# Key sums joined to the attention visit of the unit ahead, and second weights split a step sooner

## Chip, cores and metric

The kernel runs on one core of one Trainium2 chip. The metric is the time of one execution on the device in microseconds; a kernel's time is the median of its runs. Beside the times there is one profiled execution, and all views of the profile come from it.

## What is computed

An attention block with a polynomial sketch, and behind it a mixture of four experts. The essence of the reference:

```python
def phi(x):                       # x: (4, 4, 1088, 32)
    a = np.einsum('rd,bhsd->bhsr', S1, x)       # r = 8
    b = np.einsum('rd,bhsd->bhsr', S2, x)
    return np.einsum('bhsi,bhsj->bhsij', a, b).reshape(*x.shape[:-1], 64)
q_p, k_p = phi(q), phi(k)
kv = np.einsum('bhsf,bhsd->bhfd', k_p, v)
z = np.sum(k_p, axis=2)
attn = np.einsum('bhsf,bhfd->bhsd', q_p, kv) / (np.einsum('bhsf,bhf->bhs', q_p, z)[..., None] + 1e-6)
x = attn.transpose(0, 2, 1, 3).reshape(4352, 128)
p = domain_probs / (domain_probs.sum(-1, keepdims=True) + 1e-9)
out = sum(p[:, e:e+1] * (np.maximum(x @ w1[e], 0) @ w2[e]) for e in range(4))   # w1: 128 x 1024
```

All inputs and the output are float32.

## The kernel before

**The experts are the backbone.** The 4352 rows of x are cut into 11 chunks, `CHUNKS = [128, 448, 512, 448 x 7, 128]`. For each chunk `m` there are `NQ = 16` steps, four per expert `e`, each with two blocks `j` of 128 hidden columns: two half-steps per step. Half-step numbers below count all of them from the start, one for every call of `work()`. In the middle chunks a float32 product is made of float32r products of split numbers: for the first weights, `first` issues L1116 (`wa` by `xa`) and L1117 (`wb` by `xb`) into a PSUM tile `g`, ACT rescales it (L1118), and one half-step later `third` adds the third product (L1165, `wd` by `xd`); ACT then makes the hidden rows (L1168 `ha` or L1173 `hid`), and VectorE their low parts (`lower`: L1142 `hb`, L1145 `hd`). Products with the second weights follow some half-steps later in an order written out by hand (`DEAL`; L1233, or L1214 in chunk 1, where experts 0 and 1 take plain float32 second weights; there expert 0 also takes plain float32 first weights, L1103). The first and last chunk are plain float32, in halves of the array.

**Splits of weights.** `weight_parts(e)` splits the first weights in four parts: ACT splits half of `w1` into `wa` and VectorE joins `wb`; VectorE makes `wd`; and the same for the other half. `second_weight_parts(e)` has two parts: in each, ACT makes one split of 128 x 768 (`vab`) and VectorE two joins. `vab` takes the buffer in which `w1` of the same expert was. The dictionary `to_part` says after which steps a part is issued: first weights of experts 1, 2, 3, 0 from steps 12, 13, 16, 19 on, second weights from steps 32, 17, 20, 23 on, one part per step. What is issued after a step stands on ACT's and VectorE's queues behind that step's own instructions, and each engine works its queue in order.

**The attention is filled in between.** Batch 0's keys come first (`start`). The rest is a plan, a list of pieces with a cost, a name and a distance: a piece such as `("product", 3)` may not run sooner than three half-steps after the piece named `product`. In every half-step `work()` adds to a credit, at a rate that has each chunk's rows ready in time, and runs pieces while there is credit. A counter `holds` says that a PSUM tile is held for the plan; while it isn't zero, every half-step has credit for one piece. All PSUM tiles of the plan and all `g` come from one pool of six banks in turn (`ps_h`).

**Units.** A batch's rows of queries are cut into units, `UNITS = [[128, 448, 512], [448, 448, 192], [256, 448, 384], [512, 320, 256]]`; unit (b, u) is the u-th of batch b. A unit `w` passes through these pieces: a transpose of its queries (`unit_turn`); in the *visit* of the unit before it, the projection with the sketch (`unit_project`: eight matmuls in halves of the array, an ACT copy, two stores to DRAM and four loads back, all on SP's queue); two products on VectorE (`unit_product`); its own visit, in which TensorE makes numerators and denominators (`unit_visit`, `attend_products`: 16 to 32 matmuls in halves of the array, from `qp` and `kvx`); then on VectorE inverse, scale and output, and by DMA the rows go to x.

**Keys.** For each batch `key_pieces` lays 13 pieces: three transposes, three times a projection (TensorE) and its sum (VectorE; the last one also requests keys and values of the next batch), and four products (VectorE, 128 x 576). `key_end` adds two: `keysum`, three half-steps behind the last product, in which `key_sum` adds up `kv` over nine tiles of rows for two pairs of heads, 72 matmuls in halves of the array; and `keyblocks`, in which VectorE makes `kvx` from `kv`. All units of the batch need `kvx`. In `lay_plan` the 13 pieces of batches 1 to 3 are dealt out over the units, by the table `at`: for batch 2, pieces 5 to 12 stand ahead of unit (2, 0), and for batch 3 pieces 9 to 12 ahead of unit (3, 0); `key_end(b)` follows ahead of unit (b, 0).

The helpers `on_side` and `both` issue one matmul on one half of the array's columns, alternating; all of these matmuls are recorded under L236, those of the full-width key projections under L430.

Of the kernel before, what the change touches and what calls it, by code (L numbers as in the profile page):

```python
# [17 lines left out]
def _ap(t, p0: int, np_: int, off: int, free):  # L18

    p = list(t.ap)[0]  # L20
    return bass.AP(t.tensor, t.offset + p0 * p[0] + off, [[p[0], np_]] + [list(d) for d in free])
# [3 lines left out]
def kernel(  # L25
# [28 lines left out]
    B, H, S, D = q.shape  # L54
# [23 lines left out]
    UNITS = [[P, 448, 512], [448, 448, 192], [256, 448, 384], [512, 320, 256]]  # L78
# [10 lines left out]
    ps_h = ctx.enter_context(tc.tile_pool(name="ps_h", bufs=6, space=bass.MemoryType.PSUM))  # L89
# [4 lines left out]
    def psum(pool, tag):  # L94
        return pool.tile([P, 512], F32, tag=tag, name=tag)
# [142 lines left out]
    def both(out, weights, moving, **flags):  # L238

        for _ in range(2):  # L240
            on_side(lambda s: out[half[s], :], lambda s: weights[:, half[s]], lambda s: moving, **flags)
# [200 lines left out]
    def key_product(b, t0, n, p, x, eng, kf=None):  # L442

        if b:
            fs = lambda k, dims: _ap(fss[b], 0, P, 32 * (NT * p + t0) + R2 * x + k, [[32, n]] + dims)
            eng.tensor_tensor(
                out=_ap(kps[b], 0, P, 256 * t0 + P * p + R * x, [[256, n], [R2, R], [1, R]]),
                in0=fs(0, [[1, R], [0, R]]), in1=fs(R, [[0, R], [1, R]]), op=ALU.mult,
            )
            return  # L450
        src, off = (kf, P * p) if kf is not None else (fss[b], 32 * (NT * p + t0))
        eng.tensor_tensor(
            out=_ap(kps[b], 0, P, 256 * t0 + P * p + 64 * x, [[256, n], [32, 2], [R, 4], [1, R]]),
            in0=_ap(src, 0, P, off + 4 * x, [[32, n], [R2, 2], [1, 4], [0, R]]),
            in1=_ap(fss[b], 0, P, 32 * (NT * p + t0) + R, [[32, n], [R2, 2], [0, 4], [1, R]]),
            op=ALU.mult,
        )

    def key_sum(b, p, kv, t0=0, n=NT):
        for t in range(t0, t0 + n):  # L460
            both(
                kv[:, 256 * p : 256 * p + 2 * (D + 1)],
                kps[b][:, t, p, :],
                vx[:, t, 2 * p : 2 * p + 2].rearrange("p h d -> p (h d)"),

                start=(p == t == 0),
                stop=(t == NT - 1),
                skip_group_check=True,
            )
# [13 lines left out]
    def key_blocks(b, kv):  # L483

        kvx[b] = apool.tile([P, 2, 2 * (D + 1)], F32, tag="kvx", bufs=2, name="kvx")
        nc.vector.tensor_tensor(
            out=_ap(kvx[b], 0, P, 0, [[2 * (D + 1), 2], [D + 1, 2], [1, D + 1]]),
            in0=_ap(kv, 0, P, 0, [[256, 2], [D + 1, 2], [1, D + 1]]),
            in1=_ap(own8, 0, P, 0, [[0, 2], [32, 2], [0, D + 1]]) if b else _ap(own2, 0, P, 0, [[0, 2], [1, 2], [0, D + 1]]),
            op=ALU.mult,  # L490
        )

    holds = [0]

    def held(x):
        holds[0] += 1
        return x

    def free():
        holds[0] = 0  # L500

    def key_pieces(b):

# [18 lines left out]
        for p in range(2):  # L522
            for x in range(2):
                add(0.76, lambda p=p, x=x: key_product(b, 0, NT, p, x, nc.vector), "products")

    def key_end(b):

        kv = []

        def sums():  # L530
            kv.append(held(psum(ps_h, "h")))
            for p in range(2):
                key_sum(b, p, kv[0])

        def blocked():
            key_blocks(b, kv[0])
            free()

        add(0.1, sums, "keysum", ("products", 3))
        add(0.29, blocked, "keyblocks", ("keysum", 1))  # L540

    def unit_parts(b, c, n):

# [118 lines left out]
    def banks_of(laid):  # L662

        tiles = sum(T[0] for _, T, _ in laid)
        return tiles, [(i, 3 * i, min(tiles, 3 * i + 3)) for i in range((tiles + 2) // 3)]
# [14 lines left out]
    def attend_scale(nd, laid, rc):  # L680

        xs = apool.tile([P, QW], F32, tag="qT", name="xs")
        banks = banks_of(laid)[1]
        for i, t0, t1 in banks:
            nc.vector.tensor_tensor(
                out=_ap(xs, 0, P, P * t0, [[D, H * (t1 - t0)], [1, D]]),
                in0=_ap(nd[i], 0, P, 0, [[D + 1, H * (t1 - t0)], [1, D]]),
                in1=_ap(rc, 0, P, H * t0, [[1, H * (t1 - t0)], [0, D]]),
                op=ALU.mult,
            )  # L690
        free()
        return xs

    def attend_out(b, c, n, laid, xs):
# [41 lines left out]
    turned, factors, products, over = {}, {}, {}, {}  # L736

    def unit_turn(w):

        b, c, n, u = later[w]  # L740
        turned[w] = query_turn(b, c, n)
        if u == len(UNITS[b]) - 1 and b + 1 < B:
            load_rows(q, b + 1, "qn")
# [34 lines left out]
    def unit_product(w, p):  # L778

        n, (qp, qb) = later[w][2], factors[w]  # L780
        nc.vector.tensor_tensor(out=qp[p][:, 0:n], in0=qp[p][:, 0:n], in1=qb[p][:, 0:n], op=ALU.mult)

    def unit_visit(w):

        b, c, n, _ = later[w]
        products[w] = attend_products(b, c, n, factors.pop(w)[0])

    def unit_out(w):

        b, c, n, _ = later[w]  # L790
        for _ in attend_out(b, c, n, products.pop(w)[1], over.pop(w)):
            pass

    def vector_us(n):

        return 0.16 + n * 1.04e-3

    plan = []

    def add(cost, run, name, after=None):  # L800

        plan.append((cost, run, name, after))

    def lay_plan():

        of_first = queries(0, P, UNITS[0][1])
        costs = [0.62] * 9 + [0.05] * 4 + [0.4, 0.55, 0.6, 0.1, 0.1]
        distances = {12: ("first8", 3), 13: ("first12", 1), 16: ("first15", 2), 17: ("first16", 2)}
        for at, cost in enumerate(costs):
            add(cost, lambda: next(of_first, None), f"first{at}", distances.get(at))  # L810
        covers.append((len(plan), P + UNITS[0][1]))
        add(vector_us(later[0][2]), lambda: unit_turn(0), "qturn", ("start", 2 * NQ - 2))
        add(0.1, lambda: unit_project(0), "visit", ("qturn", 6))
        add(0, lambda: None, "wait", ("start", 2 * NQ + 2))
        keys = {}
        for b in range(1, B):
            now_on, plan[:] = list(plan), []
            key_pieces(b)
            keys[b], plan[:] = list(plan), now_on
        for w, (b, c, n, u) in enumerate(later):  # L820
            if b == 0:
                plan.extend(keys[1][:9])
            else:
                at = {(1, 0): (1, 9, 13), (1, 1): (2, 0, 3), (1, 2): (2, 3, 5), (2, 0): (2, 5, 13)}
                at.update({(2, 1): (3, 0, 3), (2, 2): (3, 3, 9), (3, 0): (3, 9, 13)})
                if (b, u) in at:
                    k, z0, z1 = at[b, u]
                    plan.extend(keys[k][z0:z1])
                if u == 0:
                    key_end(b)  # L830
            more = w + 1 < len(later)
            if more:
                add(vector_us(later[w + 1][2]), lambda w=w: unit_turn(w + 1), "qturn")
            for p in range(2):
                add(vector_us(n), lambda w=w, p=p: unit_product(w, p), "product", ("visit", LAND if w else LAND + 1))

            def visit(w=w, more=more):
                if more:
                    unit_project(w + 1)
                unit_visit(w)  # L840

            add(0.1, visit, "visit", ("product", 3))
            add(0.4, lambda w=w: inverse.__setitem__(w, attend_inverse(*products[w])), "inverse", ("visit", 1))
            add(vector_us(n), lambda w=w: over.__setitem__(w, attend_scale(*products[w], inverse.pop(w))), "scale")
            add(vector_us(n), lambda w=w: unit_out(w), "out")
            covers.append((len(plan), S * b + c + n))
# [439 lines left out]

    start()
    lay_plan()
    place, now, at_of, credit, spent = [0], [0], {"start": 0}, [0.0], [0.0]

# [35 lines left out]
        begun_hp[i] = psum(ps_h, "h")  # L1326
        half_columns(i, begun_hp[i], 0)
    to_part = {}
    for e, at, then in zip((1, 2, 3, 0), (12, 13, 16, 19), (32, 17, 20, 23)):
        for at, parts_of in ((at, weight_parts(e)), (then, second_weight_parts(e))):  # L1330
            for step in range(at, at + 4):
                to_part.setdefault(step, []).append(parts_of)
    for m in range(1, NC - 1):
        at, tokens = NQ * m - 4 if m > 1 else NQ + 1, token_parts(m)
# [132 lines left out]
```

## Time and profile before

| what | value |
|---|---|
| median of 3 runs | 452.62 us (452.27 to 453.0) |
| profiled execution | 452.55 us |
| its span, first to last instruction | 450.6 us |
| instructions | 8662 |
| key-sum matmuls of the third batch | 72, 174.34 us to 176.59 us |
| key-sum matmuls of the fourth batch | 72, 265.62 us to 267.87 us |
| visit of unit (1, 2) | from 148.68 us |
| visit of unit (2, 2) | from 241.43 us |
| ACT splits of second weights, experts 2, 3, 0 | 34.78, 38.38; 45.48, 48.39; 56.27, 58.98 us |

The costliest groups of the page, with engine, operation, tiles written and read, shape and count, then busy time in us, mean ns of one, and the engine's idle time before them with what ended it:

```profile
L1118 ACT ACTIVATE h<-h 128x448 f32<-128x448 f32 (+1 forms) x280 | 151.4, 541 | 77.5 <-PE h L1117 72.3
L1142 DVE SCALAR_TENSOR_TENSOR hb<-h,ha 128x448 fp32r<-128x448 f32 (+1 forms) x204 | 125.8, 624 | 51.2 <-ACT ha L1168 50.2
L1116 PE MATMUL h<-xa,wa 128*128 128x448 f32 (+1 forms) x280 | 130.3, 465 | 0.0
L1165 PE MATMUL h<-xd,wd 128*128 128x448 f32 (+1 forms) x280 | 103.5, 370 | 0.6 <-ACT h L1118 0.6
```

PE is TensorE, PEld its weight loads, DVE VectorE, ACT ScalarE, POOL GpSimd, SPq the queue of the SyncE engine, which issues most DMAs. TensorE has no idle time ahead of its matmuls to speak of; their lengths are modelled and overlap, so distances from start to start say more than lengths.

### The profile page before, as it was taken

To read this page: it belongs to the slowest core of one execution; us is meant where nothing else is said; L and a number is where in the kernel's file an instruction comes from. 1 tells how busy PE (TensorE), PEld (TensorE's weight loads), DVE (VectorE), ACT (ScalarE), POOL (GpSimd) and SP (SyncE) were. 2 spreads that over 40 slices of the span, in tenths; PEclk is the share of its full clock that TensorE was granted. 3 is DMA by queue.
4 is the path that set the end of the run, shared out by engine and by line. 5 is a ranking of instruction groups with operands and counts; after the bars stand their busy time and mean duration, and the time that the engine had idled before them with its cause. 6 is when DMAs were issued, how large, how long until landed. Compare 5 with 4: busy or idle time off the path is not lost.

```text
span 450.6 us, 8662 instructions
## 1 busy us (share of the span) xinstructions
PE 445.1 (99%) x3013; PEld 367.7 (82%) x3013; DVE 359.4 (80%) x606; ACT 330.7 (73%) x699; POOL 120.3 (27%) x206
## 2 busy tenths in 40 slices
PE   8999999999999999999999999999999999999997
PEld 5876678777778888888888888888888888888886
DVE  5897689887988788889877988787779787787753
ACT  4267788677867786778687867788778788877741
POOL 7352133211323123212321332124123212321320
PEclk9999999999999999999999999999999999999999
DMA  7944741014223251152243501410421121017401
GB/s 198 315 127 141 192 137 38 25 35 123 93 60 86 80 131 23 38 129 74 72 115 60 126 22 31 119 49 21 92 54 31 32 45 41 21 37 231 141 2 28
DMA packets 53779, 38.45 MB, mean 85 GB/s; under 512 B 26920, under 2 KB 49896, under 8 KB 53736
## 3 DMA queue, kind: packets, MB, share of 16 engines
q1 hardware_dynamic: 53064, 37.77, 31.3%
q8 instruction: 23, 0.38, 0.3%
q14 instruction: 20, 0.16, 0.1%
q0 software_dynamic: 448, 0.07, 0.1%
q10 hardware_dynamic: 224, 0.07, 0.1%
HBM read 32.68 MB, written 5.21 MB: 84 GB/s over the span
## 4 chain that ended last, share of the span: by engine, by line
PE 93%; DVE 3%; ACT 2%; DMA 1%; issue 1%; SPq 0%; ACTq 0%; DVEq 0%
PE o L1233 40%; PE h L1165 13%; PE h L1116 13%; PE h L1117 13%; PE h L236 7%; PE o L236 3%; PE o L1214 2%; PE h L1103 1%; DMA vn<-in_v_dram 1%; PE h L430 1%; DVE qp L582 1%; ACT h L1118 1%; ACT vab L888 0%; DVE qa L864 0%; ACT hid L1173 0%
## 5 line engine op out<-in xcount | busy, mean ns | idle before, releaser
L1118 ACT ACTIVATE h<-h 128x448 f32<-128x448 f32 (+1 forms) x280 | 151.4, 541 | 77.5 <-PE h L1117 72.3
L1142 DVE SCALAR_TENSOR_TENSOR hb<-h,ha 128x448 fp32r<-128x448 f32 (+1 forms) x204 | 125.8, 624 | 51.2 <-ACT ha L1168 50.2
L1116 PE MATMUL h<-xa,wa 128*128 128x448 f32 (+1 forms) x280 | 130.3, 465 | 0.0
L1145 DVE SCALAR_TENSOR_TENSOR hd<-ha,hb 128x896 fp32r<-128x896 f32 (+1 forms) x102 | 116.4, 1141 | 8.5 <-PE h L1117 0.5
L1168 ACT ACTIVATE ha<-h 128x448 fp32r<-128x448 f32 (+1 forms) x204 | 111.7, 548 | 0.0
L1165 PE MATMUL h<-xd,wd 128*128 128x448 f32 (+1 forms) x280 | 103.5, 370 | 0.6 <-ACT h L1118 0.6
L1117 PE MATMUL h<-xb,wb 128*128 128x448 f32 (+1 forms) x280 | 103.0, 368 | 0.0
L1272 POOL TENSOR_TENSOR ev<-ev,gate 128x256 f32<-128x256 f32 (+1 forms) x54 | 39.9, 739 | 219.6 <-DVE ev L1265 201.5
L1233 PE MATMUL o<-ha,vab 128*128 128x448 f32 (+1 forms) x204 | 76.5, 375 | 0.0
L1117 PEld LDWEIGHTS h<-xb,wb 128*128 128x128 f32 x280 | 52.7, 188 | 18.7 <-issue 14.8
L1116 PEld LDWEIGHTS h<-xa,wa 128*128 128x128 f32 x280 | 52.7, 188 | 18.7 <-issue 14.3
L1233 PE MATMUL o<-hid,w_sb 128*128 128x448 f32 (+1 forms) x136 | 63.0, 545 | 0.0
L1165 PEld LDWEIGHTS h<-xd,wd 128*128 128x128 f32 x280 | 52.5, 187 | 9.2 <-ACT h L1118 2.6
L1233 PE MATMUL o<-hd,vd 128*128 128x448 f32 (+1 forms) x204 | 58.9, 369 | 0.0
L1233 PE MATMUL o<-hb,vb 128*128 128x448 f32 (+1 forms) x136 | 50.0, 369 | 0.0
L1274 POOL TENSOR_TENSOR total<-total,ev 128x256 f32<-128x256 f32 (+1 forms) x54 | 47.3, 876 | 4.2
L1173 ACT ACTIVATE hid<-h 128x448 f32<-128x448 f32 (+1 forms) x76 | 42.2, 555 | 0.1
L1233 PEld LDWEIGHTS o<-ha,vab 128*128 128x128 f32 x204 | 38.3, 188 | 4.2 <-issue 0.2
L1233 PEld LDWEIGHTS o<-hd,vd 128*128 128x128 f32 x204 | 38.1, 188 | 3.5
L1272 POOL TENSOR_TENSOR total<-ev,gate 128x256 f32<-128x256 f32 (+1 forms) x18 | 12.8, 731 | 78.4 <-issue 58.3
L1233 PEld LDWEIGHTS o<-hid,w_sb 128*128 128x128 f32 x136 | 25.5, 188 | 2.5 <-DVE ev L1265 0.3
L1233 PEld LDWEIGHTS o<-hb,vb 128*128 128x128 f32 x136 | 25.5, 188 | 2.0
(142 smaller groups left out, 452.5 us busy)
## 6 DMA issues: line engine op xcount, KB each, us to landing
gate<-gates SPq DMA_DIRECT2D x24, 224.0 KB
kn<-in_k_dram SPq DMA_DIRECT2D x4, 544.0 KB
vn<-in_v_dram SPq DMA_DIRECT2D x16, 128.0 KB
w_last<-in_moe_w_dram SPq DMA_DIRECT2D x4, 512.0 KB
w_sb<-in_moe_w_dram SPq DMA_DIRECT2D x3, 512.0 KB
w_sb<-in_moe_w_dram SPq DMA_DIRECT2D x6, 256.0 KB
qp<-qd SPq DMA_DIRECT2D x6, 224.0 KB
qb<-qd SPq DMA_DIRECT2D x6, 224.0 KB
```

Of the source, the lines that this page charges most:

```text
L236: nc.tensor.matmul(out(s), weights(s), moving(s), **flags)
L1116: nc.tensor.matmul(g, wa[:, e, w], xa, start=True, stop=False)
L1117: nc.tensor.matmul(g, wb[:, e, w], xb, start=False, stop=True)
L1118: nc.scalar.activation(g, g, ACTF.Copy, scale=1.0 + R12)
L1142: nc.vector.scalar_tensor_tensor(out=hb, in0=g, scalar=0.0, in1=high, op0=ALU.max, op1=ALU.subtract)
L1145: nc.vector.scalar_tensor_tensor(out=d2, in0=a2.bitcast(F32), scalar=R12, in1=b2.bitcast(F32), op0=ALU.mult, op1=ALU.subtract)
L1165: nc.tensor.matmul(g, w, x, start=False, stop=True, skip_group_check=True)
L1168: nc.scalar.activation(ha, g, ACTF.Relu, scale=NEAR)
L1173: nc.scalar.activation(hid[i][j], g, ACTF.Relu)
L1233: nc.tensor.matmul(acc[m, e][o][:, 0:n], w, h, start=first_one, stop=last)
L1272: nc.gpsimd.tensor_tensor(out=to[:, x], in0=ev[:, x], in1=g[:, x], op=ALU.mult)
L1274: nc.gpsimd.tensor_tensor(out=total[m][:, x], in0=total[m][:, x], in1=ev[:, x], op=ALU.add)
```

## The change

Four things are changed.

1. `free` takes a number: it lowers `holds` by that much instead of setting it to zero; `attend_scale` gives back as many as it has tiles.
2. For batches 2 and 3 the remaining key pieces (5 to 12 of batch 2, 9 to 12 of batch 3) stand behind the products of the last unit of the batch ahead, (1, 2) or (2, 2), and ahead of its visit; that visit waits for three half-steps behind the last key product.
3. The key sums of these batches are made inside that visit, ahead of the next unit's projection and of the unit's own products; `keyblocks` follows one half-step behind the visit, ahead of the unit's inverse. Batch 1 stays as it was.
4. The second weights of experts 2, 3 and 0 are split from steps 16, 19 and 22 on instead of 17, 20 and 23.

```diff
-    def free():
-        holds[0] = 0
+    def free(n=1):
+        holds[0] = max(0, holds[0] - n)
...
+    sums = {}
+
+    def key_sums(b):
+        sums[b] = held(psum(ps_h, "h"))
+        for p in range(2):
+            key_sum(b, p, sums[b])
+
     def key_end(b):
 
-        kv = []
-
-        def sums():
-            kv.append(held(psum(ps_h, "h")))
-            for p in range(2):
-                key_sum(b, p, kv[0])
-
         def blocked():
-            key_blocks(b, kv[0])
+            key_blocks(b, sums.pop(b))
             free()
 
-        add(0.1, sums, "keysum", ("products", 3))
-        add(0.29, blocked, "keyblocks", ("keysum", 1))
+        if b == 1:
+            add(0.1, lambda: key_sums(b), "keysum", ("products", 3))
+        add(0.29, blocked, "keyblocks", ("keysum" if b == 1 else "visit", 1))
...
-        free()
+        free(len(nd))
         return xs
...
-                at = {(1, 0): (1, 9, 13), (1, 1): (2, 0, 3), (1, 2): (2, 3, 5), (2, 0): (2, 5, 13)}
-                at.update({(2, 1): (3, 0, 3), (2, 2): (3, 3, 9), (3, 0): (3, 9, 13)})
+                at = {(1, 0): (1, 9, 13), (1, 1): (2, 0, 3), (1, 2): (2, 3, 5), (2, 1): (3, 0, 3), (2, 2): (3, 3, 9)}
                 if (b, u) in at:
                     k, z0, z1 = at[b, u]
                     plan.extend(keys[k][z0:z1])
-                if u == 0:
+                if b == 1 and u == 0:
                     key_end(b)
...
-            def visit(w=w, more=more):
+            last = 0 < b < B - 1 and u == len(UNITS[b]) - 1
+            if last:
+                plan.extend(keys[b + 1][(5, 9)[b - 1] :])
+
+            def visit(w=w, more=more, then=b + 1 if last else None):
+                if then:
+                    key_sums(then)
                 if more:
                     unit_project(w + 1)
                 unit_visit(w)
 
-            add(0.1, visit, "visit", ("product", 3))
+            add(0.1, visit, "visit", ("products" if last else "product", 3))
+            if last:
+                key_end(b + 1)
...
-    for e, at, then in zip((1, 2, 3, 0), (12, 13, 16, 19), (32, 17, 20, 23)):
+    for e, at, then in zip((1, 2, 3, 0), (12, 13, 16, 19), (32, 16, 19, 22)):
         for at, parts_of in ((at, weight_parts(e)), (then, second_weight_parts(e))):
```

## The prediction

> **What bounds the kernel.** I read the page first: the busy shares, then the chain of waits.
>
> ```profile
> PE 445.1 (99%) x3013; PEld 367.7 (82%) x3013; DVE 359.4 (80%) x606; ACT 330.7 (73%) x699; POOL 120.3 (27%) x206
> PE 93%; DVE 3%; ACT 2%; DMA 1%; issue 1%; SPq 0%; ACTq 0%; DVEq 0%
> ```
>
> The first line is busy time, the second the chain that ended last. TensorE is the chain for 93% of the span, at a granted clock of 1.00 in every stretch I asked for between 16 and 430 us. So a change is worth what it does to the spacing of matmuls, and a stall of another engine counts where TensorE has to wait for it. A "busy" TensorE still hides spacing losses, so the next view is its timeline round one of the key sums that move (start, length, engine, what).
>
> ```profile
> 265.32 0.37 PE L1165 MATMUL h<-xd,wd 128*128 128x448 f32 x1
> 265.62 2.32 PE L236 MATMUL h<-vx,kp 128*64 128x66 f32 x72
> 267.87 0.47 PE L1233 MATMUL o<-ha,vab 128*128 128x448 f32 x1
> 268.18 0.36 PE L1233 MATMUL o<-hb,vb 128*128 128x448 f32 x1
> ```
>
> Undisturbed products of 448 columns start every 0.20 us (265.12, 265.32). Here the step into the insert is 0.30, the insert takes 2.25 (265.62 to 267.87), and the first step behind it is 0.31 instead of 0.20. Two visits, the last one and that of unit (2, 2), show what is fixed in an insert:
>
> ```profile
> 351.56 0.69 PE L236 MATMUL h<-kvx,qp 128*64 128x66 f32 x16
> 352.18 0.47 PE L1233 MATMUL o<-ha,vab 128*128 128x448 f32 x1
> ...
> 241.43 1.08 PE L236 MATMUL h<-qT,sx 128*64 128x256 f32 x8
> 242.35 0.87 PE L236 MATMUL h<-kvx,qp 128*64 128x66 f32 x24
> 243.15 0.47 PE L1233 MATMUL o<-ha,vab 128*128 128x448 f32 x1
> ```
>
> 16 matmuls of the same shape take 0.62 us, 72 take 2.25: (2.25 − 0.62) / 56 = 0.029 each, and 0.62 − 16 × 0.029 = 0.16 that does not depend on their number. An insert thus costs 0.10 + 0.11 + 0.15 = 0.36 beside its own streaming.
>
> **The merge, part by part.** Removed: two inserts of key sums (at 174.34 and 265.62) as inserts of their own. Their 72 matmuls each remain, now ahead of the projection in the visits of (1, 2) and (2, 2). Saved per batch are the fixed 0.36, less what the new joint inside the visit costs. A joint between projection and products exists already: the visit of (2, 2) takes 243.15 − 241.43 = 1.72, its 24 products 0.16 + 24 × 0.029 = 0.86, so the 8 projection matmuls take 0.86, 0.108 each; 256 columns at four passes, two halves of the array together, are 0.107 by the same reckoning that makes 128 columns 0.054 (visit at 148.68). The joint is below 0.01. From both sides: 0.36 saved at most, and at least the 0.20 of the two edges, should the 0.15 come back at the joint. I take 0.35, the joint being the nearest row. Two batches: **−0.70 us**, bounds −0.72 and −0.40.
>
> What moves with them. Working the planner's costs and distances through for both plans, half-step by half-step, nothing differs before the visit of (1, 2). That visit goes from half-step 111 to 125, the last key product of its batch from 127 to 122, kvx from 131 to 126, the output of (1, 2) from 114 to 130; in the next batch the visit goes from 177 to 189, the last product from 192 to 186, the output from 181 to 194. Later visits stay within one half-step. Needs: tokens of the chunk that uses the outputs of (1, 2) and (2, 0) are split at half-step 152, and (2, 0) leaves at 142 in both plans, so the later output of (1, 2) costs nothing; for (2, 2) the same, since (3, 0) leaves at 209 in both.
>
> DMAs: the visit of (1, 2) issues its eight transfers on SP over 149.75 to 154.80, so 6 us from the visit's start. The next product waits for them: at half-step 134, nine after the visit, 9 × 1.25 = 11 us (eight undisturbed half-steps take 10.03 us, 374.14 to 384.17) plus the insert. Cover some 5 us; without it VectorE would wait in order, with the next hb behind it, and TensorE for that. The gate transfer of chunk 4, which left at 172.63, is next on SP and leaves about 2 us later; its user comes some ten half-steps on. The keys and values of the fourth batch are requested five half-steps sooner, with no wait in sight. Nothing moves on POOL.
>
> PSUM: six banks in turn. The visit takes kv, qc and one nd, so the bank that kvx must free is needed again three half-steps after the visit and kvx is computed one after it; nd is needed after six and scaled after two or three. Nothing waits, by the order; at zero.
>
> VectorE is where cover is thin. Between half-steps 177 and 189 the visit of (2, 2) used to give VectorE a rest.
>
> ```profile
> 240.00:250.00 10.00, 10.00 (x72) 8.46 (x71) 7.48 (x14) 7.21 (x16) 0.75 (x2) 1.00 0.49 103
> 250.00:257.00 7.00, 7.00 (x35) 6.08 (x34) 6.60 (x10) 6.30 (x15) 2.82 (x3) 1.00 0.54 116
> ```
>
> (Columns: window, TensorE, its weight loads, VectorE, ACT, POOL busy.) VectorE idles 2.52 + 0.40 = 2.92 there. The change takes 1.72 + 0.36 = 2.08 of TensorE time out, and swaps work of the same size: inverse, scale and transpose of (2, 2) go (0.16 + 0.23 + 0.56 + 0.57 = 1.52), two key products come (2 × 0.75 = 1.50). Cover left: 0.84 us. I cost it at nothing; if the idle cannot be used it costs up to 2.08. For (1, 2) the idle of 150 to 170 is 3.18 + 1.04 against 1.41 removed: wide.
>
> The trace has one key product of 1.19 us against 0.75, at 63.51, where POOL was multiplying gates (63.49). The Trainium skill, "SBUF — State Buffer", section "SBUF: two separate sides", says that VectorE with two SBUF inputs and GpSimd hold a shared port pair exclusively, the later one waiting for the whole instruction. That row agrees; by the rule every moved product that starts while POOL multiplies would wait, which is what rival 4 below would come from.
>
> **The second weights.** Before, ACT's split of second weights for experts 2, 3, 0 comes at steps 17, 20, 23, each in two parts; after, at 16, 19, 22. What counts is where two ACT splits meet. Before, step 21 has one (expert 3, part two, 0.87) and a first-weight split of expert 0 (0.66) back to back:
>
> ```profile
> 43.07 0.64 ACT L888 ACTIVATE wa<-w_sb 128x512 fp32r<-128x512 f32 x1
> 43.60 0.54 ACT L1118 ACTIVATE h<-h 128x448 f32<-128x448 f32 x1
> ...
> 48.39 0.87 ACT L888 ACTIVATE vab<-w_sb 128x768 fp32r<-128x768 f32 x1
> 49.12 0.66 ACT L888 ACTIVATE wa<-w_sb 128x512 fp32r<-128x512 f32 x1
> 49.64 0.58 ACT L1118 ACTIVATE h<-h 128x448 f32<-128x448 f32 x1
> ```
>
> ```profile
> 49.59 0.37 PE L1117 MATMUL h<-xb,wb 128*128 128x448 f32 x1
> 50.27 0.47 PE L1165 MATMUL h<-xd,wd 128*128 128x448 f32 x1 [0.32 <-ACT h L1118]
> ```
>
> The third product comes 0.68 after the second instead of 0.20: a stall of 0.48. After the change step 21 has the 0.66 alone: **−0.48**. A second such stall, 0.44, stands at 60.98 to 61.62, behind the split that ACT ran at 58.98 (step 24). That split goes a step ahead; the rescale L1118 there is then held only by the copy L1262, which can start at about 60.40 and frees ACT at 60.81, instead of 61.01: **−0.20**.
>
> But step 19 now has both: part one of expert 3 (0.73 to the next ACT start, as 48.39 to 49.12) ahead of expert 0's first split (0.52, 49.12 to 49.64). ACT reaches them at 43.07, bound by TensorE's products before, so L1118 starts at 43.07 + 0.73 + 0.52 = 44.32, not 43.60. Its third product was due at 44.36 and comes 0.63 after the start (49.64 to 50.27): 44.95, a new stall of **+0.60**. The first split at step 16 must also wait for VectorE's join of the same expert's first weights (32.20 to 32.88), as it writes over their buffer; ACT stands till 32.9, and qs leaves 0.55 late. The hidden rows behind it are used three half-steps later, so TensorE doesn't notice. At step 22 the split waits for a join behind the query product that a DMA releases at 51.42; ACT is free again at about 53.5 to 54.1, and L1118 is needed at 54.6, because the visit at 52.04 holds TensorE. Sum: −0.48 − 0.20 + 0.60 = **−0.08**. Bounds: −0.92 (both stalls go, no new one) and +0.60 (new one, the old ones just move).
>
> **Sum.** −0.70 − 0.08 = −0.78. The profiled span of 450.6 becomes 449.8; its execution took 452.55, 1.95 round the span, which stays. Against the median of 452.62: **451.8 us**.
>
> **Rivals.**
> 1. Both ACT stalls go and the one at step 19 does not come (the value copies and the last key copy, 42.45 to 43.07, would have to be done sooner): −0.70 − 0.92, 451.0. For it: ACT idles 1.06 ahead of 42.01. Against: that idle ends on TensorE.
> 2. The merge does only part of what it says: the 0.15 returns at the joint, −0.40 − 0.08, 452.1. Against it: the joint inside visits.
> 3. The ACT stall only moves, +0.60 − 0.70, 452.5. For it: ACT is busy 9.35 of 10 us between 42 and 52.
> 4. The other side: VectorE becomes the bound between half-steps 177 and 189. Its idle of 2.92 stands largely in one wait for ACT behind the visit (2.02 before 245.28), which goes with the visit; if the rest is unusable, TensorE waits 2.08 for hb. It decides as soon as usable idle is under 2.08; two products as long as the one at 63.51, 0.44 more each, would bring it there. Against it: the idle of 2.92, and all eight products of these two batches took 0.75 us. 452.62 − 0.78 + 2.08 = 453.9.
>
> **How the numbers follow.** What a measurement of this kernel can tell from no change is about 0.2%, 0.9 us. Forecast 48%, a third of it beyond −0.9 with the spread of the runs (452.27 to 453.0) and a few tenths in the stalls; its own range 451.3 to 452.3. Rival 1: 22%; rival 2: 10%; rival 3: 10%; rival 4 and the like: 10%. Faster: 16 + 22 = 38%; slower 10%; the rest, 52%, within. The range takes the bounds −1.62 and +0.20, some 0.2 of spread on each: 450.8 to 453.0; rival 4 and a part of rival 1 stay out.
>
> **What would show it.** Right: between matmuls round 174 and 265 no insert of 72 alone; one insert of 72 + 8 + 16 near 167 and one of 72 + 8 + 24 near 256, with one 0.30 and one 0.31 at their ends; the stall at 49.6 gone and a gap L1117 to L1165 of about 0.8 near 44.2. Wrong: the 0.2 edges twice inside the visit; waits of TensorE on VectorE's hb between 244 and 256; L1165 at 44.36 as before; a wait on the transfers of qb behind the merged visits.

## The result and the profile after

The change takes the median from 452.61 us (452.27 to 453.0) to **451.47 us** (451.19 to 451.69), nine executions each on one chip: ratio 0.9975, interval [0.9965, 0.9985]. In two further comparisons the pair was 452.63 and 451.63 (0.9986 [0.9972, 1.0]; one of the twelve executions took 455.56) and 452.47 and 451.32 (0.9974 [0.9964, 0.9985]). So the gain is 1.0 to 1.15 us, about 0.25%. The profiled span goes from 450.6 to 449.6, and the end of TensorE's last matmul from 447.30 to 446.33.

The busy times of the page after (busy time, share of the span, number of instructions):

```profile
PE 443.5 (99%) x3013; PEld 367.4 (82%) x3013; DVE 359.0 (80%) x606; ACT 330.6 (74%) x699; POOL 120.0 (27%) x206
```

The number of matmuls is the same, 3013; TensorE is still busy for 99%, and the span is 1.0 shorter. As foretold, the page cannot say where that is from; the spacing of the matmuls can. So the main reading is a subtraction: for each half-step, the start of its first matmul in the trace after, less its start in the trace before. A place where that offset changes is a place where time was won or lost. The changed kernel was profiled three times, once in each comparison.

| place (half-steps) | forecast | after, first profile | second | third |
|---|---|---|---|---|
| start-up, until the first expert matmul (28.47 us before) | 0 | −0.04 | −0.08 | −0.06 |
| second weights (41 to 54) | −0.08 | −0.08 | −0.09 | −0.08 |
| first merge (110 to 131) | −0.35 | −0.52 | −0.51 | −0.52 |
| second merge (177 to 196) | −0.35 | −0.36 | −0.34 | −0.36 |
| end of TensorE's work | −0.78 | −0.97 | −0.89 | −1.02 |

What a row doesn't hold is scatter of up to 0.12 between these places.

**The merged inserts** in TensorE's timeline after (start, length, engine, line, what; the key sums have 72 matmuls, the projection 8, the products 16); the first of the two:

```profile
166.52 0.37 PE L1173 MATMUL h<-xd,wd 128*128 128x448 f32 x1
166.82 2.32 PE L236 MATMUL h<-vx,kp 128*64 128x66 f32 x72
168.97 0.61 PE L236 MATMUL h<-qT,sx 128*64 128x128 f32 x8
169.41 0.64 PE L236 MATMUL h<-kvx,qp 128*64 128x66 f32 x16
169.97 0.47 PE L1241 MATMUL o<-ha,vab 128*128 128x448 f32 x1
170.28 0.37 PE L1241 MATMUL o<-hb,vab 128*128 128x448 f32 x1
```

One step in of 0.30 (166.52 to 166.82), one step out of 0.31 (169.97 to 170.28), nothing lost at the joints inside. The body is 3.15 long (166.82 to 169.97); that of the second insert, at 255.87 with 24 products, 3.82, with steps of 0.29 and 0.31. In the profile before, the key sums took 2.25 and the two visits 1.05 (from 148.68) and 1.72, so 3.30 and 3.97 apart. Each body is 0.15 shorter, and one pair of edges, 0.20, is gone: 0.35 each time, the forecast's own two terms.

**The second weights.** ACT and TensorE after, where the new stall was foretold:

```profile
43.05 0.86 ACT L896 ACTIVATE vab<-w_sb 128x768 fp32r<-128x768 f32 x1
43.80 0.63 ACT L896 ACTIVATE wa<-w_sb 128x512 fp32r<-128x512 f32 x1
44.32 0.54 ACT L1126 ACTIVATE h<-h 128x448 f32<-128x448 f32 x1
```

```profile
44.14 0.37 PE L1125 MATMUL h<-xb,wb 128*128 128x448 f32 x1
44.91 0.47 PE L1173 MATMUL h<-xd,wd 128*128 128x448 f32 x1 [0.40 <-ACT h L1126]
45.22 0.54 PE L1222 MATMUL o<-hid,w_sb 128*128 128x448 f32 x1
```

Two ACT splits now stand ahead of the rescale L1126, which starts at 44.32, so the third product comes 0.77 after the second, not 0.20. The product behind it is late once more: it follows 0.31 on (44.91 to 45.22), not 0.20, as it did behind the old stall (50.27 to 50.59 before). So the new stall costs 0.57 + 0.11 = 0.68. The same timeline has the stall of 49.6 gone (L1125 at 48.90, L1173 at 49.10), and the one at 61 smaller (61.06 to 61.53; 0.64 before).

### The profile page after: what moved, and what is told of

Same layout as the page of the kernel before. It is cut to its first block, busy times and chain, and to the rows that moved or that the text cites. A ratio compares the mean times of both kernels' runs of the same rounds, so it can differ in the third digit from the quotient of the medians.

```text
span 449.6 us, 8655 instructions
## 1 busy us (share of the span) xinstructions
PE 443.5 (99%) x3013; PEld 367.4 (82%) x3013; DVE 359.0 (80%) x606; ACT 330.6 (74%) x699; POOL 120.0 (27%) x206
## 4 chain that ended last, share of the span: by engine, by line
PE 94%; DVE 3%; DMA 1%; ACT 1%; issue 0%; SPq 0%; DVEq 0%
PE o L1241 40%; PE h L1173 13%; PE h L1124 13%; PE h L1125 13%; PE h L236 7%; PE o L236 3%; PE o L1222 2%; PE h L1111 1%; PE h L430 1%; DMA kn<-in_k_dram 1%; DVE qp L583 1%; DMA vn<-in_v_dram 0%; ACT h L1126 0%; DVE qa L872 0%; DVE rd L615 0%
## 5 line engine op out<-in xcount | busy, mean ns | idle before, releaser
L1126 ACT ACTIVATE h<-h 128x448 f32<-128x448 f32 (+1 forms) x280 | 151.3, 540 | 74.0 <-PE h L1125 69.5
L1173 PE MATMUL h<-xd,wd 128*128 128x448 f32 (+1 forms) x280 | 103.5, 370 | 0.5 <-ACT h L1126 0.4
L1125 PE MATMUL h<-xb,wb 128*128 128x448 f32 (+1 forms) x280 | 103.1, 368 | 0.0
L1280 POOL TENSOR_TENSOR ev<-ev,gate 128x256 f32<-128x256 f32 (+1 forms) x54 | 40.9, 757 | 219.4 <-DVE ev L1273 201.7
L1125 PEld LDWEIGHTS h<-xb,wb 128*128 128x128 f32 x280 | 52.7, 188 | 18.8 <-issue 14.8
L1173 PEld LDWEIGHTS h<-xd,wd 128*128 128x128 f32 x280 | 52.5, 187 | 9.2 <-ACT h L1126 2.6
L1282 POOL TENSOR_TENSOR total<-total,ev 128x256 f32<-128x256 f32 (+1 forms) x54 | 46.1, 853 | 4.2
```

The source lines that it names most:

```text
L1125: nc.tensor.matmul(g, wb[:, e, w], xb, start=False, stop=True)
L1126: nc.scalar.activation(g, g, ACTF.Copy, scale=1.0 + R12)
L1173: nc.tensor.matmul(g, w, x, start=False, stop=True, skip_group_check=True)
L1280: nc.gpsimd.tensor_tensor(out=to[:, x], in0=ev[:, x], in1=g[:, x], op=ALU.mult)
L1282: nc.gpsimd.tensor_tensor(out=total[m][:, x], in0=total[m][:, x], in1=ev[:, x], op=ALU.add)
```

## The experiments

Eight runs, each with five rounds beside the kernel before on the same chip. The first four shared one chip (before: 452.37, 452.05 to 452.81).

### The merge without the split, and the split without the merge

```diff
 # the changed kernel, first run
-    for e, at, then in zip((1, 2, 3, 0), (12, 13, 16, 19), (32, 16, 19, 22)):
+    for e, at, then in zip((1, 2, 3, 0), (12, 13, 16, 19), (32, 17, 20, 23)):
 # the kernel before, second run
-    for e, at, then in zip((1, 2, 3, 0), (12, 13, 16, 19), (32, 17, 20, 23)):
+    for e, at, then in zip((1, 2, 3, 0), (12, 13, 16, 19), (32, 16, 19, 22)):
```

> The merge alone, the second weights split at steps 17, 20, 23 as before. Theory (the merge gives two times 0.35 us of edges and, by the way, a wait of 0.22 us of TensorE for an accumulator near 169.8 goes; the split gives 0.09): 451.7 us, the end 0.87 us ahead of before, with the stalls of 0.48 at 49.6 and 0.44 at 61 back and none at 44. Rival (the merge gives the forecast 0.70 or less and the rest of the 1.14 comes from the split): 451.9 to 452.2, the end 0.4 to 0.7 ahead.

> Only the second weights a step sooner, the key sums as before. Theory: the stall at 49.6 goes (0.48), the one at 61 shrinks by 0.2, a new one of 0.60 stands at 44: 452.5 us, the end 0.1 us ahead of before. Rival (the split gives the part of the gain that was not forecast): 452.2 to 452.3.

The merge alone: 451.66, ratio 0.9983 [0.9974, 0.9992]. The split alone: 452.42, ratio 0.9999 [0.999, 1.0008]. By offsets: the merge wins 0.51 between half-steps 110 and 131 and 0.36 between 177 and 196; its start-up ended 0.18 later than that of before, which is why its span is 449.9. The split alone loses 0.69 up to half-step 43, has 0.59 of it back by 47 and another 0.18 by 54: −0.08, and nothing behind that. Counted from the end of the start-up to TensorE's end, the merge wins 0.93 and the split 0.05, against 0.81 to 0.95 in the three profiles of the change. So by the offsets the parts add up, and nearly all of the gain is the merge. The medians don't confirm this by themselves: 0.71 for the merge and −0.05 for the split, beside 1.00 to 1.15 for the change on other chips; the intervals, some 0.4 to each side, cover the difference. With the split alone the second and third product stand at 44.27 and 45.04, the same gap of 0.77 as in the change; with the merge alone they are 0.20 apart there. It is the split that makes the new stall.

### The key sums moved, but not joined

```diff
-        if b == 1:
-            add(0.1, lambda: key_sums(b), "keysum", ("products", 3))
-        add(0.29, blocked, "keyblocks", ("keysum" if b == 1 else "visit", 1))
+        add(0.1, lambda: key_sums(b), "keysum", ("products", 3) if b == 1 else ("visit", 1))
+        add(0.29, blocked, "keyblocks", ("keysum", 1))
...
             def visit(w=w, more=more, then=b + 1 if last else None):
-                if then:
-                    key_sums(then)
```

The change had a gain of 0.52 at the first merge where the two terms that can be seen in the insert make 0.35. Here the same work lies at nearly the same places in the order, but the key sums are an insert of their own again, one half-step behind the visit.

> The key sums moved as in the change, but as an insert of their own one half-step behind the visit instead of inside it. Theory (the gain is the edges of an insert saved; only the wait near 169.8 hangs on the move): two inserts more, 0.70 us slower than the changed kernel, 452.2 us, the wait near 169.8 still gone. Rival (the gain comes from where the visits and key products now lie, not from the joint): no more than 0.2 us slower than the changed kernel, 451.7 or less.

Median 452.22, ratio 0.9996 [0.9987, 1.0006]. TensorE's timeline of this kernel:

```profile
166.53 0.37 PE L1170 MATMUL h<-xd,wd 128*128 128x448 f32 x1
166.82 0.66 PE L236 MATMUL h<-qT,sx 128*64 128x128 f32 x8
...
167.88 0.47 PE L1238 MATMUL o<-ha,vab 128*128 128x448 f32 x1
...
169.20 0.36 PE L1170 MATMUL h<-xd,wd 128*128 128x448 f32 x1
169.49 2.32 PE L236 MATMUL h<-vx,kp 128*64 128x66 f32 x72
171.74 0.47 PE L1238 MATMUL o<-ha,vab 128*128 128x448 f32 x1
```

Both inserts have their own step in (0.29 each) and step out (the next products start at 168.19 and 172.05, 0.31 on), and their bodies are 1.06 and 2.25, 3.31 together, against the joined 3.15. By offsets this kernel wins 0.16 at the first place (−0.09 to −0.25) and nothing at the second (−0.23 before and behind it). Against the change it lacks 0.36 at each of the two. So the joining is worth 0.36 per batch, and the first place has 0.16 more that comes from the new order alone.

The Trainium skill says in "TensorEngine Tiling (Array Packing)", section "Key Properties", that a change of the tiling mode drains TensorE; it gives no time for it. The runs agree in that nothing is lost between key sums, projection and products, which all use half the array's columns, while each pair of changes to and from the full-width matmuls costs 0.35; that it is a drain which takes this time, no run shows.

The profile before sets one rival aside: that any insert of plain float32 matmuls costs as much. The key projections of L430 are such an insert at full width, of 8 matmuls at 154.09 and of 2 at 157.76:

```profile
154.09 1.05 PE L430 MATMUL h<-sk,kT 128*128 128x128 f32 x8
154.90 0.45 PE L1233 MATMUL o<-ha,vab 128*128 128x448 f32 x1
```

From the product ahead of the insert to the second one behind it, 153.89 to 155.19 and 157.56 to 158.19, 1.30 and 0.63 pass. Less the two steps of 0.20 that products take anyway, the inserts cost 0.90 and 0.23: 0.112 for each matmul, and 0.01 that is fixed. By the same count the key sums (2.46 for 72 matmuls) and the last visit (0.83 for 16) have 0.36 fixed. So the fixed cost goes with the half-width matmuls, not with every insert.

### Where the other 0.16 comes from

The half-step at 168.84 in the profile before is 1.43 long, where its like after the change is 1.21. VectorE and TensorE of before there:

```profile
168.08 1.09 DVE L1145 SCALAR_TENSOR_TENSOR hd<-ha,hb 128x896 fp32r<-128x896 f32 x1 [0.46 <-PE h L1117]
169.09 0.61 DVE L1265 TENSOR_TENSOR ev<-ev,o 128x448 f32<-128x448 f32 x1
```

```profile
169.44 0.37 PE L1233 MATMUL o<-ha,vab 128*128 128x448 f32 x1
169.76 0.30 PEld L1233 LDWEIGHTS o<-hid,w_sb 128*128 128x128 f32 x2 [0.33 <-DVE ev L1265]
169.76 1.02 PE L1233 MATMUL o<-hid,w_sb 128*128 128x448 f32 x2
```

The first product into an accumulator for the next expert may only start once VectorE has read the old sum out of it (L1265). VectorE has that read behind an `hd` of 1.09, and ends it at 169.70; TensorE waits, and 0.32 lie between two products that follow at 0.20. The `hd` itself was late: VectorE stood idle for 0.46 ahead of it, which the profile puts down to TensorE's L1117 of 167.61. Of the 102 `hd` in this profile it is the only one with such a wait, and the run with the split alone has it again. After the change, VectorE:

```profile
166.24 1.09 DVE L1153 SCALAR_TENSOR_TENSOR hd<-ha,hb 128x896 fp32r<-128x896 f32 x1
167.25 0.61 DVE L1273 TENSOR_TENSOR ev<-ev,o 128x448 f32<-128x448 f32 x1
```

Two things are different. VectorE's order has changed, and `hd` no longer waits for TensorE: it starts 0.47 behind the first product of its half-step (165.77 to 166.24), where it was 1.02 behind before (167.06 to 168.08). And the visit stands just ahead of the hand-over, and holds TensorE's products from 166.82 to 169.97. The read ends at 167.86, and TensorE's next use of that accumulator, at 171.70, is 0.20 behind the product ahead of it.

That the new order removes the wait is shown: the three profiles of the change, the merge alone and the run with the parts moved but not joined all have `hd` without the idle time, and the last also wins the 0.16. Which of the two does it is open, as either would do. Without the visit, TensorE would have come to the accumulator near 168.35 (an estimate: the first product of the half-step at 165.77, and 2.58 from there as in the profile before with a step of 0.20), and the read would still have been 0.49 ahead. With the visit, a read that ended 0.55 later, as before, would still have been more than 3 ahead of 171.70. Why `hd` waited in the old order the rows don't tell. The size differs by a few hundredths (0.22 in the half-step, 0.16 in the offset, as some 0.06 is given back in the half-steps round it).

### The splits of second weights at 16, 20 and 22

```diff
-    for e, at, then in zip((1, 2, 3, 0), (12, 13, 16, 19), (32, 16, 19, 22)):
+    for e, at, then in zip((1, 2, 3, 0), (12, 13, 16, 17), (32, 16, 20, 22)):
```

This moves expert 0's first weights two steps ahead and expert 3's second weights back to step 20, so that from step 19 on no step has two of ACT's splits (16 and 17 do).

> The changed kernel with the ACT splits dealt out so that no step from 19 on has two: first weights of expert 0 from step 17 instead of 19, second weights of experts 2, 3, 0 from 16, 20, 22. Theory (each stall there is two ACT splits back to back ahead of the rescale L1118): no stall at 44, none at 49.6, about 0.2 left at 61: 0.6 us ahead of the changed kernel, 450.9 us. Rival (VectorE, busy 12.7 of 14 us between 28 and 42, takes the two more joins badly, and key projections or tokens come late): a wait of TensorE on VectorE between 34 and 45, 451.3 or more.

Median 451.33, ratio 0.9976 [0.9966, 0.9985]: level with the change. The new stall of 44 us is away, but the offset is +0.69 already at half-step 41 (0.06 of it from the start-up), and back at −0.02 by 54. TensorE of this kernel, then VectorE of the same:

```profile
40.03 1.13 PE L430 MATMUL h<-sk,kT 128*128 128x128 f32 x8 [0.39 <-DVE kT L392]
```

```profile
37.78 0.69 DVE L899 SCALAR_TENSOR_TENSOR wb<-w_sb,wa 128x512 fp32r<-128x512 f32 x1
...
39.18 0.70 DVE L387 STREAM_TRANSPOSE kT<-kn 128x512 f32<-128x512 f32 x1
```

A second, short transpose follows at 39.80; after the change the two start at 38.48 and 39.11. In VectorE's order a join of first weights (`wb`) now stands ahead of them, and TensorE's key projection has to wait: the rival of the expectation. The stall had only changed its engine.

### One split a step from step 19 on, without crowding the transposes

```diff
-            for step in range(at, at + 4):
+            for step in (18, 19, 21, 22) if (e, at) == (0, 19) else range(at, at + 4):
```

Expert 0's first weights are split at steps 18 and 21 here. Step 18, like 16, still has two of ACT's splits; this costs nothing that the trace shows (the offset is +0.07 at the end of the start-up and +0.09 at half-step 41).

> First weights of expert 0 split at steps 18, 19, 21 and 22 (in the change 19 to 22), second weights at 16, 19 and 22 as in the change, so that no step from 19 on holds two of ScalarE's splits. If the stall near 44 us comes from the two splits of step 19 standing ahead of L1126 (L1126 at 44.32 against the 43.60 of before): L1126 starts near 43.8, L1173 is at most 0.05 late, the rest lies as after the change, and the end comes 0.5 to 0.6 earlier: span 449.0 to 449.1, median about 450.9 beside the change's 451.4. Rival: the join that VectorE now does at step 18 makes it late for the turns of the keys, TensorE waits for VectorE between 38 and 41 as it did with the splits at 17, 20 and 23 replaced by 16, 20 and 22, and the median stays at 451.3.

> The change itself, on the same chip as the kernel with one split a step, to compare the two directly: span 449.6, median 451.4 by the earlier runs. If its first merge is worth 0.53 and its second 0.35 as in the first profile, the distance to the kernel before in TensorE's order grows by 0.53 between half-steps 110 and 131 and by 0.35 between 131 and 196 again; if the 0.18 that the first has over the second was an accident of that execution, it is 0.35 both times.

Medians 451.44 and, for the change, 451.63; ratios to before 0.9975 [0.9966, 0.9984] and 0.9986 [0.9972, 1.0]. The 450.9 that was expected did not come. In the trace the theory of the stall holds. ACT of this kernel:

```profile
43.16 0.86 ACT L896 ACTIVATE vab<-w_sb 128x768 fp32r<-128x768 f32 x1
43.91 0.55 ACT L1126 ACTIVATE h<-h 128x448 f32<-128x448 f32 x1
```

One split ahead of the rescale, not two, and the third product at 44.50 is 0.06 late. Between half-steps 41 and 54 this kernel wins 0.61 where the change wins 0.08. From the end of the start-up to TensorE's end it is ahead of before by 1.33 (0.93 and 0.81 in the change's first two profiles). So the trace says 0.4 to 0.5 better, and the medians 0.19, within their intervals. A repeat of both, on another chip, was to settle that:

> The kernel with one split a step once more, beside the change once more. In the first profiles it stood 0.40 to 0.51 ahead of the change, counted from the end of the start-up, but the medians were only 0.19 apart with overlapping intervals. If the trace tells the truth for most executions: median some 0.3 to 0.5 below the change's on the same chip. Rival: the 0.4 is spent by start-up loads and other scatter in most executions, and the medians lie within 0.1.

> The change itself beside it: median 451.4 to 451.6, first merge 0.50 to 0.53 and second 0.34 to 0.36 in its trace as in the profiles so far.

It did not. Medians 451.33 and 451.32; ratios 0.998 [0.9968, 0.9991] and 0.9974 [0.9964, 0.9985]. The eleven executions of the kernel with one split a step fall apart: five at 450.70 to 451.03, three at 451.33 to 451.64, three at 452.68 to 452.86. The change's eight lie at 451.22 to 451.42, with one at 452.09. The profiled execution of the repeat was one of the late ones (span 450.9). In it, the window in question wins 0.59 again (+0.65 at half-step 41, +0.06 at 54). Its time was lost elsewhere: the start-up ended 0.61 late, ahead of anything the edit touches, and TensorE stood for ACT near 70 us, ACT itself for a transfer of tokens:

```profile
69.83 0.63 ACT L896 ACTIVATE xa<-ring 128x512 fp32r<-128x512 f32 x1 [0.84 <-DMA ring<-xd]
```

The rescale behind it, L1126, starts at 70.36, and TensorE's next product at 70.94. In this execution SP issued that transfer at 66.99, in the nine other profiles at 64.95 to 66.14; SP had waited 1.5 for keys from memory earlier. That cost 0.97 of offset between half-steps 60 and 70. Whether a kernel that reaches this place half a microsecond sooner meets the transfer more often, or this chip had three unlucky executions, is open. So one split a step is not shown to beat the change.

## Why the prediction was right, point by point

- **The bound and the way of counting.** Right: spacing of matmuls and nothing else. 451.8 was forecast, 451.3 to 451.6 measured, inside the likeliest case's own range of 451.3 to 452.3. The sum was −0.78, and the traces have −0.89 to −1.02, of which 0.04 to 0.08 is start-up.
- **The edges and the fixed part, −0.35 per batch.** Right in both terms (0.20 and 0.15, in both inserts). The joint does cost nothing, so rival 2, the 0.15 coming back there, is out; the apart run puts the joining at 0.36 per batch.
- **The term that was mis-sized** is the merge at half-steps 110 to 131: 0.35 forecast, 0.52 measured. The prediction looked at what the moved visit might make TensorE wait for, and costed it at nothing; it did not look at what waited in the profile before at the place to which the visit goes. A wait of TensorE for VectorE's accumulator read stood there, at 169.76, and with the new order it is gone, which is worth 0.16.
- **The second weights.** −0.08 forecast, −0.08 to −0.09 measured in five profiles. The places were right: L1126 at 44.32 to the hundredth; its third product at 44.91 (44.95); the stall at 49.6 gone; the one at 61 smaller by 0.17 (0.20). Two of the three terms were too small: +0.68 for the new stall (+0.60) and −0.60 for the old one (−0.48), as the prediction left out the 0.11 by which the product behind a stalled one is late too. It left it out in both, and the two errors cancel; that the sum is right to a hundredth is luck. Rival 1, no new stall at all, is out in the change; rival 3, the stall merely moving at a net +0.60, is out too: the stalls at 44 and 49.6 do trade places, but at +0.08, and the one at 61 shrinks. Rival 1's result needs other steps for the first weights, and the run with one split a step shows the window at −0.61 and −0.59. At step 22 ACT was free a little sooner than forecast (53.39; 53.5 to 54.1), and nothing was late.
- **VectorE's cover of 0.84, costed at nothing.** Right: in the windows that the prediction used, after the change (TensorE, weight loads, VectorE, ACT, POOL busy):

```profile
240.00:250.00 10.00, 10.00 (x48) 8.60 (x47) 8.92 (x14) 8.14 (x18) 3.42 (x4) 1.00 0.20 20
250.00:257.00 7.00, 7.00 (x66) 5.87 (x66) 6.79 (x11) 6.32 (x14) 0.46 (x1) 1.00 0.25 33
```

VectorE is idle for 1.08 + 0.21 = 1.29 of 17 us, against 2.92 before (0.84 were forecast to be left); no wait of TensorE is recorded between 244 and 257. The margin is thin but was not spent, so rival 4 did not come: the eight moved key products, 153.80 to 253.38, took 742 to 759 ns each. None of them started while POOL was multiplying gates. Where the two met, POOL started 0.16 later and it was POOL that took longer, 1.18 and 1.19 at 157.43 and 246.42, against 0.72 at 61.12. The row at 63.51 does not stand for every such start, either: two key products of the profile before, at 73.89 and 260.36, started some 0.14 ahead of the recorded end of a POOL multiplication and took 0.756 and 0.754; records of POOL are rough.
- **The transfers, costed at nothing.** Right. The merged visit's transfers (six, two stores and four loads; the prediction counts eight) leave SP from 170.81 to 176.82, and VectorE's product that needs them starts at 184.31 without a wait.
- **The chances.** The likeliest case was called "within 0.2%" with 52% and faster with 38%. The measured 0.25% lies just beyond that bound; the intervals reach across it. The 0.16 of the unseen wait is about half of the way from the forecast −0.82 to the measured −1.14.

## What to carry to other kernels

An insert of half-array matmuls among full-width ones cost a fixed amount beside its work (here 0.35 us: two edges and a fixed part); join such inserts where their distances allow it. When an insert is moved, look at the profile not only for what it may delay, but for which waits stand in its new surroundings. Count a stall to the product behind the stalled one. Where ACT was nearly full (9.35 of 10 us between 42 and 52 before), two splits in one step made TensorE wait, and two in steps 16 or 18 did not; lay such jobs one to a step where there is no room, and check each other engine that the earlier one feeds.

## What was not expected of the hardware

Two executions of one kernel differ by as much as the edits here are worth: the end of the start-up lay between 0.08 us ahead of that of before and 0.61 behind it (nine profiles), and one late token transfer cost 0.97 in a single execution. The first product of 448 columns after a break is followed 0.29 to 0.32 on, not 0.20, whether the break was a half-array insert (169.97 to 170.28), a full-width one (154.90 to 155.19) or a wait (44.91 to 45.22). ACT's successive instructions overlap: a split of 0.86 us is followed by the next start after 0.75 (43.05 to 43.80), and the shorter one of 0.63 after 0.52, so the delay of a queued instruction is to be summed from starts, as the prediction did, and not from durations.
